# A planner's estimates and constants set anew in an attention and feed-forward kernel on one core

## The chip, the cores and the metric

The kernel runs on one core of a Trainium2 chip. A core has TensorE (PE, matmuls; PEld is its weight load), VectorE (DVE), ScalarE (ACT), GpSimd (POOL) and SyncE (SP), whose queue issues every DMA of this kernel. The metric is the device time of one execution in microseconds (us); lower is better.

## What is computed

```python
# B, H, Sl, Sg, D = 8, 8, 512, 32, 64
k_all, v_all = concat([k_g, k_l]), concat([v_g, v_l])
out_g = softmax(q_g @ k_all.T / 8) @ v_all                 # 32 global queries see everything
s_ll  = q_l @ k_l.T / 8, where |i - j| <= 32, else -1e9    # local queries: a window
out_l = softmax([q_l @ k_g.T / 8, s_ll]) @ v_all           # and the 32 global keys
x = concat([out_g, out_l]).reshape(B * 544, 512)
h = x @ w_in                                               # 512 -> 2048
g = h * tanh(softplus(h))                                  # mish
return g @ w_out                                           # 2048 -> 512
```

Everything is float32 outside. Inside, most products are made from two 16-bit or reduced parts (high and low), so that one float32 product is three matmuls (hi x hi, hi x lo, lo x hi).

## The kernel before

**Tiling.** Batches go from 0 to 7, head pairs (hp) from 0 to 3 in each, and four tiles of 128 queries (t) in each pair: 128 attention units. A unit computes scores `s` (two matmul groups, one for each head), the masked row maximum `P, nm` (DVE, L614), the exponential (ACT, L623), a high and a low part `ph` (ACT or DVE, L307, and DVE, L642), a DMA transpose to `pt` (SP, L467), and the product with v, `U` (PE, L659). After four units `x` (DVE, L669) is normalised, split into `xs` and transposed by DMA into `xh` and `xl`, which hold a whole batch. Each head pair also has the global queries: `g`, `gmx`, `gP`, `gph`, `gpt`, `gu`.

The feed-forward part works on blocks of 256 rows (two for each batch) in eight steps each: `h` (PE, L788, 24 matmuls, two halves of 12), mish into `e` (ACT, L831), two 16-bit parts `G` (DVE, L309 and L844), and `o` (PE, L856, 12 matmuls). Both h and o need prepared weights.

**The weights' way in.** The weights arrive as 64-bit words, 32 tiles of 512 KB: 0 to 15 are w_in, 16 to 31 w_out. Each is loaded (`w_load`) into a free place (`wraw` in a tile that is not yet in use, or a row of `W`). `w_bits` and `w_sum` make float32 from it: DVE shifts (L384), ACT takes the low word to `wr` (L386), DVE ors (L393), POOL adds (L395). `w_stat` multiplies each tile by itself on PE (`ws`, L405). After 16 tiles `w_norm` reduces: DVE `wd, wm` (L412), POOL's all-reduce `wp` (L416), DVE, ACT Ln and Exp (L418, L419), DVE scales `iw, sw`. Then `w_split` makes high and low parts of each of eight tiles: scaling (L307 or L309), high part, low part, the last on DVE for five tiles (L440) and on POOL for the other eleven (L445).

**The order.** Nothing is issued as it is written. Every step is added to a planner with its engine, an estimate of its time and a priority; `order` runs a list schedule over these estimates, and the instructions are then issued in the order of the estimated starts, one fixed queue for each engine. An engine takes what can start first, and of those ready the one of least priority number. A step's number is its place in the program, plus `late`, or `PER` = 37 times a `slot` where one is given. Estimates and constants thus set nothing on the chip but the order. Waits on the chip are for semaphores only, so a step that is late holds all that is queued behind it on its engine.

The constants of the weights' way in are slots: `CONV1 + RATE1 * k` and `CONV2 + RATE2 * (k - 16)` for the conversion of tile k, `AHEAD_DMA` by how many slots its load goes before it, `FIRST` and `STEP` for the splits. `LATE_K`, `LATE_L`, `LATE_B` and `LATE_V` push back the keys, the loads of k and q, the attention, and the values of batch 1.

Of the kernel before, what the change touches and what calls it, by code (L numbers as in the profile page):

```python
# [50 lines left out]
class Plan:  # L51
# [81 lines left out]
    def order(self):  # L133
        N = len(self.tasks)
        left, users = [0] * N, [[] for _ in range(N)]
        for n, t in enumerate(self.tasks):
            both = t[2] | t[3]
            left[n] = len(both)
            for d in both:
                users[d].append(n)  # L140
        free = dict.fromkeys((PE, DVE, ACT, POOL, DMA), 0)
        queue = {e: [] for e in free}
        start, done, on = [None] * N, [0] * N, [None] * N
        columns = {}

        def tensor(t, ns, rows):

            while ns > 1e-6:
                k = int(t / self.TICK + 1e-9)
                slow = 1 if columns.get(k - 1, 0) >= self.COLUMNS else 2  # L150
                d = min(ns * slow, (k + 1) * self.TICK - t)
                columns[k] = columns.get(k, 0) + d / slow * 2.4 * rows
                ns -= d / slow
                t += d
            return t

        def enter(n):
            engs, fn, deps, after, new, pri, rows, table = self.tasks[n]
            for e, ns in engs:
                t = max([done[d] + (self.NEXT[e] if on[d] == e else self.HOP) for d in deps] + [start[a] for a in after] + [0])  # L160
                bisect.insort(queue[e], (pri, n, ns, t))

        def first(e):

            best = None
            for pri, n, ns, t in queue[e]:
                t = max(t, free[e]) + (self.TABLE if e == ACT and self.tasks[n][7] not in (None, self.table) else 0)
                e0 = self.tasks[n][0][0][0]
                if e0 != e and free[e0] <= t + self.LOYAL:
                    continue  # L170
                if best is None or t < best[0]:
                    best = (t, pri, e, n, ns)
                    if t == free[e]:
                        break
            return best

        for n in range(N):
            if not left[n]:
                enter(n)
        for _ in range(N):  # L180
            t, pri, e, n, ns = min(c for c in map(first, free) if c)
            start[n], on[n] = t, e
# [32 lines left out]
def attn_mish_kernel(ctx: ExitStack, tc: tile.TileContext, qt, kt, qt0, kt0, vm, vg, qg, w1, w2, consts_in, out, w64):  # L215
# [73 lines left out]
    def pool(cols):  # L289
        return 2.39 * cols  # L290
# [38 lines left out]
    def wh(j, hl):  # L329
        return W[:, j + j // 8, hl * 512:(hl + 1) * 512].bitcast(F16)  # L330
# [26 lines left out]
    def words(k):  # L357
        return raw(k).rearrange("p (f w) -> p f w", w=2)
# [21 lines left out]
    def w_bits(k):  # L380
        if not w64:
            return
        f, key = lambda: wf(k).bitcast(I32), wkey(*HV[k])
        pl.add(DVE, 335, lambda: V.tensor_scalar(f(), words(k)[:, :, 1], 3, 0x3FFFFFFF, ALU.logical_shift_left, ALU.bitwise_and),  # L384
               r=[rawkey(k)], w=[key])
        pl.add(ACT, act(512), lambda: A.activation(out=X["wr", k], in_=words(k).bitcast(U32)[:, :, 0], func=AF.Copy,  # L386
                                                   scale=2.0 ** -29), r=[rawkey(k)], new=[("wr", ("wr", k))])

    def w_sum(k):
        if not w64:  # L390
            return
        f, key = lambda: wf(k).bitcast(I32), wkey(*HV[k])
        pl.add(DVE, 602, lambda: V.scalar_tensor_tensor(f(), words(k)[:, :, 1], -0x40000000, f(), ALU.bitwise_and, ALU.bitwise_or),  # L393
               r=[rawkey(k)], w=[key])
        pl.add(POOL, pool(512), lambda: G.tensor_tensor(f(), f(), X["wr", k], ALU.add), r=[("wr", k)], w=[key])  # L395

    def w_stat(k):

# [10 lines left out]
    def w_norm(w):  # L409

        m, p = ("wm", w), ("wp", w)
        pl.add(DVE, 210, lambda: V.tensor_tensor_reduce(out=X["wd", w][:, 0, :128],  # L412
                                                        in0=X["ws", w][:, :128], in1=ident, scale=1.0,
                                                        scalar=0.0, op0=ALU.mult, op1=ALU.add, accum_out=X[m]),
               r=[("ws", w), "consts"], new=[("wm", m), ("ob", ("wd", w))])
        pl.add(POOL, 600, lambda: G.partition_all_reduce(X[p], X[m], 128, RED.add), r=[m], new=[("p2", p)])  # L416
        pl.add(DVE, 70, lambda: V.tensor_scalar(X[p], X[p], TINY * TINY, None, ALU.max), w=[p])
        pl.add(ACT, 94, lambda: A.activation(out=X[p], in_=X[p], func=AF.Ln, bias=0.0, scale=1.0), w=[p], table="exp")  # L418
# [13 lines left out]
    def w_split(j):  # L432

        parted.add(j)
        w = j // 8
        f, c, k = W[:, j + j // 8 + 1, :], sw[:, w:w + 1], ("W", j + j // 8 + 1)
        hi, lo = [wslot(j), "hi"], [wslot(j), "lo"]
        if j < 8 - ON_POOL:
            pl.add([(ACT, act(1024)), (DVE, dve2(1024))], 0, lambda e: scaled(e, wh(j, 0), f, c), r=[k, ["sw", w]], w=[wslot(j)])
            pl.add(DVE, dve(1024), lambda: V.scalar_tensor_tensor(wh(j, 1), f, c, wh(j, 0), ALU.mult, ALU.subtract),  # L440
                   r=[k, ["sw", w], hi], w=[lo])
        else:
            pl.add([(ACT, act(1024)), (DVE, dve2(1024))], 0, lambda e: scaled(e, f, f, c), r=[["sw", w]], w=[k])
            pl.add([(ACT, act(1024)), (DVE, dve2(1024))], 0, lambda e: copy(e, wh(j, 0), f), r=[k], w=[wslot(j)])
            pl.add(POOL, pool(1024) * 0.9, lambda: G.tensor_tensor(wh(j, 1), f, wh(j, 0), ALU.subtract), r=[k, hi], w=[lo])  # L445


    LO, HI = slice(0, 64), slice(64, 128)
# [15 lines left out]

    def turn(kib, dst, src, r, w=(), new=()):

        pl.add(DMA, kib * 5, lambda: nc.sync.dma_start_transpose(dst(), src()), r=r, w=w, new=new)  # L467

    def b_load(b, what=None):
        if what == "g":  # L470
# [18 lines left out]
    def b_scale(b):  # L489

        m, p, sv = ("vmx", b), ("p2", b), ("sv", b)
        pl.add(POOL, 600, lambda: G.partition_all_reduce(X[p], X[m][:, 5:6], 128, RED.max), r=[m], new=[("p2", p)])
# [526 lines left out]
    RATE2 = 0.519  # L1019
    FIRST1 = 10.551  # L1020
    STEP1 = 0.114
    FIRST2 = 14.027
    STEP2 = 0.833
    AHEAD_DMA = 3.119
    LATE_K = 11.02
    LATE_L = 158.572
    LATE_B = 8.569
    LATE_V = 0.0

    def weights():  # L1030
        for k in range(32):
# [114 lines left out]
```

## Time and profile before

| | |
|---|---|
| time, median of 3 runs | 1021.27 us (1020.48 to 1023.16) |
| the profiled execution's own time | 1018.93 us |
| its span, first to last instruction | 1017.1 us |
| PE busy | 925.7 us, 91% |
| DVE, ACT busy | 668.5 us (66%), 680.9 us (67%) |
| POOL busy | 82.2 us, 8% |
| mean granted TensorE clock | 0.973 |
| DMA moved | 134.65 MB, of which 63.55 MB read from HBM |

A row of a timeline reads: start and length in us, engine, line, operation, output<-input, shape, count, and in brackets the idle time of the engine just before and what ended it. A row of a group ends with its count, its busy time, the mean ns of one, and the idle time before. A row of the waits gives the engine and line that waited, for whom, the sum, the number of times and the longest.

### The profile page before, as it was taken

Reading aid. Unit: us, or ns where it says so; the run is one execution under the profiler, and the core shown is the slowest. Engines: PE = TensorE matmul, PEld = TensorE weight load, DVE = VectorE, ACT = ScalarE, POOL = GpSimd, SP = SyncE. Lnnn points to the kernel's source line nnn. Section 1 sums busy time; section 2 is a strip of 40 time slices with the busy share of each in tenths; the row PEclk is TensorE's granted clock in tenths of the full one; section 3 lists DMA queues with packets and bytes.
Section 4 is the critical chain, followed back from the end, with each engine's and each line's share of the span. In section 5 each row is a group of like instructions: output and inputs, shape, how many; then the busy total and the mean of one; then the engine's idle time right before and its main releaser. Section 6 shows DMA issues by size and latency. Waiting matters only on the chain.

```text
span 1017.1 us, 20581 instructions
## 1 busy us (share of the span) xinstructions
PE 925.7 (91%) x7906; PEld 664.6 (65%) x7906; DVE 668.5 (66%) x1704; ACT 680.9 (67%) x1321; POOL 82.2 (8%) x62
## 2 busy tenths in 40 slices
PE   3455696899999999999999999999999999999996
PEld 2233475566776777677777777777777777666663
DVE  6977796887766767776677666767676655322221
ACT  3465566777897788878878888788878888211110
POOL 3725231410000000000000000000000000000000
PEclk9997588999999999999999999999999999999999
DMA  9847982587758664766557665666676544100000
GB/s 333 228 111 175 262 259 63 112 180 189 168 104 180 144 143 113 177 148 143 123 153 161 134 133 129 155 135 141 117 165 127 123 81 77 42 1 22 1 22 21
DMA packets 231802, 134.65 MB, mean 132 GB/s; under 512 B 197528, under 2 KB 209048, under 8 KB 230680
## 3 DMA queue, kind: packets, MB, share of 16 engines
q1 hardware_dynamic: 231704, 133.34, 57.1%
q8 instruction: 62, 1.02, 0.4%
q14 instruction: 36, 0.29, 0.1%
HBM read 63.55 MB, written 8.91 MB: 71 GB/s over the span
## 4 chain that ended last, share of the span: by engine, by line
PE 65%; DVE 12%; DMA 8%; ACT 4%; issue 3%; SPq 1%; POOL 0%; ACTq 0%; DVEq 0%
PE o L856 28%; PE h L788 26%; PE s L608 4%; PE U L659 3%; DMA vraw<-in_vm 3%; DMA pt<-ph 2%; PE g L697 2%; DMA gpt<-gph 2%; PE gu L745 1%; DVE vmx L481 1%; DVE P L614 1%; DVE ph L642 1%; DVE G L309 1%; SPq L296 1%; DVE kl L546 1%
## 5 line engine op out<-in xcount | busy, mean ns | idle before, releaser
L856 PE MATMUL o<-W,G 128*128 128x512 f16 x1632 | 389.8, 379 | 0.3 <-POOL W L445 0.3
L788 PE MATMUL h<-xh,W 128*128 128x256 f16 x2048 | 379.0, 275 | 5.1 <-ACT e L831 5.1
L788 PEld LDWEIGHTS <-W 128*128 128x128 f16 x3264 | 311.2, 98 | 68.6 <-issue 5.3
L788 PE MATMUL h<-xl,W 128*128 128x256 f16 x1024 | 281.0, 274 | 0.0
L856 PEld LDWEIGHTS <-G 128*128 128x128 f16 x1632 | 156.9, 98 | 144.1 <-issue 0.6
L831 ACT ACTIVATE e<-h,c 128x512 f32<-128x512 f32 (+1 forms) x137 | 92.6, 683 | 117.5 <-PE h L788 116.6
L623 ACT ACTIVATE P<-P,nm 128x192 f32<-128x192 f32 (+1 forms) x256 | 117.8, 460 | 41.5 <-DVE nm L614 40.3
L309 DVE TENSOR_SCALAR G<-e,c 128x512 f16<-128x512 f32 x129 | 63.9, 495 | 118.5 <-ACT e L831 118.4
L614 DVE CUSTOM_DVE_ANT_0 P<-s,consts 128x192 f32<-128x192 f32 (+1 forms) x256 | 90.1, 367 | 68.1 <-PE s L608 57.7
L642 DVE SCALAR_TENSOR_TENSOR ph<-P,ph 128x384 f16<-128x384 f32 (+1 forms) x128 | 78.0, 611 | 80.1 <-ACT ph L307 79.3
L844 DVE SCALAR_TENSOR_TENSOR G<-e,c,G 128x512 f16<-128x512 f32 (+1 forms) x137 | 102.0, 745 | 3.4
L831 ACT ACT_TABLE_LOAD x79 | 101.4, 1283 | 1.4
L623 ACT ACT_TABLE_LOAD x74 | 94.9, 1283 | 1.3
L659 PEld LDWEIGHTS <-pt 96*128 96x128 f16 (+1 forms) x1536 | 59.3, 101 | 33.5 <-DMA pt<-ph 26.9
L307 ACT ACTIVATE ph<-P 128x384 f16<-128x384 f32 (+1 forms) x128 | 69.7, 548 | 16.3 <-DMA pt<-ph 13.2
L659 PE MATMUL U<-va,pt 128*128 128x64 f16 (+1 forms) x768 | 59.4, 199 | 19.7 <-DMA pt<-ph 19.7
L608 PE MATMUL s<-ks,qs 128*128 128x192 f32 (+1 forms) x216 | 71.4, 353 | 1.4 <-DVE qs L538 0.9
L659 PE MATMUL U<-vc,pt 96*128 96x64 f16 x768 | 58.7, 198 | 0.0
L718 ACT ACTIVATE gP<-g,gmx 64x288 f32<-64x288 f32 x64 | 30.4, 476 | 37.5 <-DVE gmx L713 37.4
L395 POOL TENSOR_TENSOR W<-W,wr 128x512 int32<-128x512 int32 x32 | 48.8, 1535 | 79.0 <-DVE W L393 40.1
L608 PE MATMUL s<-kl,qs 128*128 128x192 f32 (+1 forms) x216 | 54.2, 274 | 0.0
L405 PE MATMUL ws<-W 128*128 128x128 bf16 x128 | 17.7, 286 | 37.4 <-POOL W L395 37.3
(103 smaller groups left out, 1024.3 us busy)
## 6 DMA issues: line engine op xcount, KB each, us to landing
kraw<-in_kt SPq DMA_DIRECT2D x27, 640.0 KB, 4.7
qraw<-in_qt SPq DMA_DIRECT2D x27, 512.0 KB, 3.8
W<-in_w SPq DMA_DIRECT2D x19, 512.0 KB, 7.1
out<-ob SPq DMA_DIRECT2D x34, 256.0 KB, 2.6
vraw<-in_vm SPq DMA_DIRECT2D x8, 1024.0 KB, 6.0
wraw<-in_w SPq DMA_DIRECT2D x13, 512.0 KB, 5.9
vc<-vf SPq DMA_DIRECT2D x32, 128.0 KB, 2.3
va<-vf SPq DMA_DIRECT2D x32, 96.0 KB, 2.3
```

Of the source, the lines that this page charges most:

```text
L307: A.activation(out=dst, in_=src, func=AF.Copy, scale=c)
L309: V.tensor_scalar(dst, src, c, None, ALU.mult)
L395: pl.add(POOL, pool(512), lambda: G.tensor_tensor(f(), f(), X["wr", k], ALU.add), r=[("wr", k)], w=[key])
L608: T.matmul(X[s][:, :w], X[qs][:, h, t * 128:(t + 1) * 128], X[k][:, h, c0:c0 + w], start=(i == 0), stop=(i == 1))
L614: pl.add(DVE, 69 + 1.04 * w, lambda: V.tensor_tensor_reduce(out=X[P][:, h, :w], in0=X[s][:, :w], in1=mask[:, m0:m0 + w], scale=-SCALE, sca ...
L623: pl.add(ACT, 160 + 0.832 * w + 93, lambda: A.activation(out=X[P][:, h, :w], in_=X[P][:, h, :w], func=AF.Exp, bias=X[nm], scale=-1.0, accu ...
L642: pl.add(DVE, dve(n), lambda: V.scalar_tensor_tensor(p_part(X[ph], t, 1), p_src(X[P], t), PSC, p_part(X[ph], t, 0), ALU.mult, ALU.subtract ...
L659: T.matmul(X[u][:, t, h, :], X[pt][:k, p * 4 + h * 2 + c, :], X[vx][:k, t, vl, h * 64:(h + 1) * 64], start=(n == 0), stop=(n == 5))
L788: T.matmul(X[h][:, f * TB:(f + 1) * TB], wh(i, wl)[:, off:off + 128], X[x][:, d, o:o + TB], start=(n == 0), stop=(n == 11))
L831: chain(blk, i, ACT, 571, lambda a, z: A.activation(out=X[e][:, a:z], in_=hv(blk, i)[:, a:z], func=AF.Mish, bias=0.0, scale=X[c][:, 0:1]), ...
L844: chain(blk, i, DVE, 602, lambda a, z: V.scalar_tensor_tensor(gp(1, blk, i)[:, a:z], X[e][:, a:z], X["c", blk][:, 2:3], gp(0, blk, i)[:, a ...
L856: T.matmul(X[o], gp(g, blk, i)[:, f, t * 128:(t + 1) * 128], wh(8 + i, wl)[:, f * 512:(f + 1) * 512], start=(i == 0 and n == 0), stop=(i = ...
```

## The change

The planner's estimates change (in ns): POOL's add of a conversion to 1400 (1224 before), its all-reduces to 4500 (600), its subtract for low parts to 2230 (2203), DVE's shift to 360 (335) and or to 680 (602), a DMA transpose to 8 for each KiB (5). A DMA's time is now counted in one stream of bytes, with up to 4 us of it ahead, in place of one transfer after the other; DVE beside a busy POOL is charged 0.6 of the overlap, not 0.5. Five constants of the weights' way in and of batch 1 change, and the loads of w_in get slots of their own. No instruction is added or removed but what follows from the order: which of ACT and DVE takes a step that either may do, and ACT's table loads, 159 before and 156 now.

```diff
-    DMA_IN, DMA_OUT, DMA_MIN = 1650, 900, 650
+    DMA_IN, DMA_OUT, DMA_MIN, DMA_AHEAD = 1300, 600, 620, 4000
...
-                ns += 0.5 * min(ns, free[POOL] - t)
+                ns += 0.6 * min(ns, free[POOL] - t)
             if e == DMA:
-                free[e] = t + max(ns, self.DMA_MIN)
-                done[n] = t + self.DMA_IN + ns + self.DMA_OUT
+                moved = max(moved, t) + ns
+                free[e] = max(t + self.DMA_MIN, moved - self.DMA_AHEAD)
+                done[n] = moved + self.DMA_IN + self.DMA_OUT
...
-        pl.add(POOL, pool(512), lambda: G.tensor_tensor(f(), f(), X["wr", k], ALU.add), r=[("wr", k)], w=[key])
+        pl.add(POOL, 1400, lambda: G.tensor_tensor(f(), f(), X["wr", k], ALU.add), r=[("wr", k)], w=[key])
...
-        pl.add(POOL, 600, lambda: G.partition_all_reduce(X[p], X[m], 128, RED.add), r=[m], new=[("p2", p)])
+        pl.add(POOL, 4500, lambda: G.partition_all_reduce(X[p], X[m], 128, RED.add), r=[m], new=[("p2", p)])
...
-    FIRST2 = 14.027
+    FIRST2 = 9.91
     STEP2 = 0.833
-    AHEAD_DMA = 3.119
-    LATE_K = 11.02
-    LATE_L = 158.572
-    LATE_B = 8.569
-    LATE_V = 0.0
+    LOAD1 = -1.233
+    LOADS1 = 0.2
+    AHEAD_DMA = 7.72
+    LATE_K = 33.326
+    LATE_L = 168.71
+    LATE_B = 9.983
+    LATE_V = 399.689
...
         if a == "w":
+            pl.slot = LOAD1 + LOADS1 * n
             w_load(n)
+            pl.slot = None
```

What this does to the order is shown at three places. In names the first index (the batch, or the block of a feed-forward step) is left out: `P_1_1` is head pair 1, unit 1 of its batch, `x_3` head pair 3; a last number only counts buffers. Line numbers of the new kernel are two higher here.

VectorE at the first weight norm, before: three steps of work stand between the reduction `wd, wm` and the row `wp` that waits for POOL's all-reduce.

```order
L393 SCALAR_TENSOR_TENSOR W<-wraw_338,W 128x512
L642 SCALAR_TENSOR_TENSOR ph_72<-P_0_2_130,ph_72 128x2x224
L412 ISA wd_400,wm_399<-ws_200,consts 128x128
L412 ISA wm_399 128x1
L614 ISA P_1_1_403,nm_1_1_0_404<-s_1_1_0_232,consts 128x224
L614 ISA nm_1_1_0_404 128x1
L614 ISA P_1_1_403,nm_1_1_1_410<-s_1_1_1_270,consts 128x224
L614 ISA nm_1_1_1_410 128x1
L642 SCALAR_TENSOR_TENSOR ph_73<-P_0_3_157,ph_73 128x2x192
L417 TENSOR_SCALAR wp_406<-wp_406 128x1
```

The same place now, right behind the rows of `wd, wm`:

```order
L644 SCALAR_TENSOR_TENSOR ph_72<-P_1_0_327,ph_72 128x4x96
L386 TENSOR_SCALAR W<-wraw_426 128x512
L616 ISA P_1_3_507,nm_1_3_0_508<-s_1_3_0_430,consts 128x192
L616 ISA nm_1_3_0_508 128x1
L395 SCALAR_TENSOR_TENSOR W<-wraw_426,W 128x512
L616 ISA P_1_3_507,nm_1_3_1_532<-s_1_3_1_449,consts 128x192
L616 ISA nm_1_3_1_532 128x1
L669 TENSOR_SCALAR rs_1_539<-sums_1_334 128x8
L670 RECIPROCAL rs_1_539<-rs_1_539 128x8
L712 TENSOR_REDUCE gmx_1_557<-g_1_0_534 64x1
L644 SCALAR_TENSOR_TENSOR ph_73<-P_1_1_406,ph_73 128x2x224
L419 TENSOR_SCALAR wp_496<-wp_496 128x1
```

A conversion, the sums `rs`, a gmx and a second ph came in between, and tiles 16 and 17 are converted ahead of `wd`, where 15 was the last.

ScalarE at the second weight norm, before: it stands behind the mish results 4 to 7 of block 0 and behind the vgf and vf of batch 1, with a table load for Ln, one for Exp and one back to mish.

```order
L831 ACTIVATE e_5_1491<-h_5_1413,c_452 128x512
L512 ACTIVATE vgf_1553<-vgraw_936,sv_1533 128x128
L307 ACTIVATE vf_0_1555<-vraw_878,sv_1533 128x4x128
L307 ACTIVATE vf_1_1574<-vraw_878,sv_1533 128x4x128
L831 ACTIVATE e_6_1578<-h_6_1493,c_452 128x512
L831 ACTIVATE e_7_1583<-h_7_1518,c_452 128x512
L418 ACT_TABLE_LOAD
L418 ACTIVATE wp_1511<-wp_1511 128x1
L419 ACT_TABLE_LOAD
L419 ACTIVATE wp_1511<-wp_1511 128x1
L307 ACTIVATE W<-W,sw 128x1024 x2
L300 CAST W<-W 128x1024
```

Now:

```order
L302 CAST qgh_1314<-qgraw_1291 128x768
L420 ACTIVATE wp_1271<-wp_1271 128x1
L720 ACTIVATE gP_0_1332,gs_0_1333<-g_0_0_1259,gmx_0_1289 64x288
L421 ACTIVATE wp_1271<-wp_1271 128x1
L720 ACTIVATE gP_0_1332,gs_0_1333<-g_0_1_1273,gmx_0_1289 64x256
L833 ACT_TABLE_LOAD
L833 ACTIVATE e_0_1359<-h_0_1276,c_609 128x512
L309 ACTIVATE W<-W,sw 128x1024
L833 ACTIVATE e_1_1387<-h_1_1299,c_609 128x512
L302 CAST W<-W 128x1024
L309 ACTIVATE W<-W,sw 128x1024
L833 ACTIVATE e_2_1425<-h_2_1369,c_609 128x512
```

The norm moved ahead of the first mish, with no table load of its own, and the splits of w_out run between the first mish results. On TensorE the first o then follows 8 half steps of h; before, it followed all of block 0 and two steps of block 1.

VectorE at the end of batch 0, before: `x_3` of batch 0 stands eight rows ahead of this piece, which holds two conversions' rows and the parts of keys 1 of batch 1 (`ks_1`, `kl_1`).

```order
L384 TENSOR_SCALAR W<-W 128x512
L614 ISA P_0_2_1171,nm_0_2_0_1172<-s_0_2_0_1159,consts 128x224
L614 ISA nm_0_2_0_1172 128x1
L393 SCALAR_TENSOR_TENSOR W<-W 128x512
L614 ISA P_0_2_1171,nm_0_2_1_1179<-s_0_2_1_1169,consts 128x224
L614 ISA nm_0_2_1_1179 128x1
L302 CAST ks_1_1185<-kraw_1_1128 128x1280
L642 SCALAR_TENSOR_TENSOR ph_73<-P_0_1_1154,ph_73 128x2x224
L546 TENSOR_TENSOR kl_1_1209<-kraw_1_1128,ks_1_1185 128x640
```

Now these parts and the low part of queries 1 stand ahead of `x_3`, which comes 23 rows behind the last row of this piece:

```order
L304 CAST ks_1_1047<-kraw_1_768 128x1280
L680 TENSOR_TENSOR xs_2_1040<-x_2_1027,xs_2_1040 128x512
L712 TENSOR_REDUCE gmx_3_1042<-g_3_1_1034 64x1
L616 ISA P_0_0_1076,nm_0_0_0_1077<-s_0_0_0_1044,consts 128x192
L616 ISA nm_0_0_0_1077 128x1
L715 TENSOR_SCALAR gmx_3_1042<-gmx_3_1042 64x1
L644 SCALAR_TENSOR_TENSOR ph_72<-P_3_2_988,ph_72 128x2x224
L548 TENSOR_TENSOR kl_1_1091<-kraw_1_768,ks_1_1047 128x640
L669 TENSOR_SCALAR rs_3_1099<-sums_3_876 128x8
L540 TENSOR_TENSOR qs_1_1031<-qraw_1_789,qs_1_1031 64x1024
```

Of the conversions, 26 stood ahead of `x_3` of batch 0 before and 31 do now. On SP's queue, 28 loads of weights stood ahead of the last transposes into `xh` of batch 0, and all 32 do now.

More of the change, by code (lines that the diff above doesn't have):

```diff
@@ L144, in order @@
         columns = {}
+        moved = 0
         def tensor(t, ns, rows):
@@ L383, in w_bits @@
         f, key = lambda: wf(k).bitcast(I32), wkey(*HV[k])
-        pl.add(DVE, 335, lambda: V.tensor_scalar(f(), words(k)[:, :, 1], 3, 0x3FFFFFFF, ALU.logical_shift_left, ALU.bitwise_and),
+        pl.add(DVE, 360, lambda: V.tensor_scalar(f(), words(k)[:, :, 1], 3, 0x3FFFFFFF, ALU.logical_shift_left, ALU.bitwise_and),
                r=[rawkey(k)], w=[key])
@@ L392, in w_sum @@
         f, key = lambda: wf(k).bitcast(I32), wkey(*HV[k])
-        pl.add(DVE, 602, lambda: V.scalar_tensor_tensor(f(), words(k)[:, :, 1], -0x40000000, f(), ALU.bitwise_and, ALU.bitwise_or),
+        pl.add(DVE, 680, lambda: V.scalar_tensor_tensor(f(), words(k)[:, :, 1], -0x40000000, f(), ALU.bitwise_and, ALU.bitwise_or),
                r=[rawkey(k)], w=[key])
-        pl.add(POOL, pool(512), lambda: G.tensor_tensor(f(), f(), X["wr", k], ALU.add), r=[("wr", k)], w=[key])
+        pl.add(POOL, 1400, lambda: G.tensor_tensor(f(), f(), X["wr", k], ALU.add), r=[("wr", k)], w=[key])
     def w_stat(k):
@@ L444, in w_split @@
             pl.add([(ACT, act(1024)), (DVE, dve2(1024))], 0, lambda e: copy(e, wh(j, 0), f), r=[k], w=[wslot(j)])
-            pl.add(POOL, pool(1024) * 0.9, lambda: G.tensor_tensor(wh(j, 1), f, wh(j, 0), ALU.subtract), r=[k, hi], w=[lo])
+            pl.add(POOL, 2230, lambda: G.tensor_tensor(wh(j, 1), f, wh(j, 0), ALU.subtract), r=[k, hi], w=[lo])
     LO, HI = slice(0, 64), slice(64, 128)
@@ L465, in turn @@
     def turn(kib, dst, src, r, w=(), new=()):
-        pl.add(DMA, kib * 5, lambda: nc.sync.dma_start_transpose(dst(), src()), r=r, w=w, new=new)
+        pl.add(DMA, kib * 8, lambda: nc.sync.dma_start_transpose(dst(), src()), r=r, w=w, new=new)
     def b_load(b, what=None):
@@ L491, in b_scale @@
         m, p, sv = ("vmx", b), ("p2", b), ("sv", b)
-        pl.add(POOL, 600, lambda: G.partition_all_reduce(X[p], X[m][:, 5:6], 128, RED.max), r=[m], new=[("p2", p)])
+        pl.add(POOL, 4500, lambda: G.partition_all_reduce(X[p], X[m][:, 5:6], 128, RED.max), r=[m], new=[("p2", p)])
         def go():
```

## The prediction

> **What bounds the kernel now.** I read the page's slices first, then busy time by stretches, then TensorE's waits, then VectorE's, and last the chain of waits and the instructions in order of time. The first fence cuts the span where the work changes character: at the first h matmul, and at the first score matmul of batch 2.
>
> ```profile
> core 0: us, PE busy (x) PEld busy (x) DVE busy (x) ACT busy (x) POOL busy (x), PEclk, DMA share, GB/s
> 0.00:132.02 132.02, 70.63 (x460) 44.31 (x461) 104.26 (x241) 69.44 (x169) 54.81 (x42) 0.84 0.82 223
> 132.02:237.29 105.27, 91.05 (x796) 66.06 (x796) 88.00 (x205) 71.28 (x141) 25.62 (x15) 0.95 0.66 152
> 237.29:1017.10 779.81, 764.03 (x6653) 554.19 (x6651) 476.21 (x1260) 540.19 (x1012) 1.75 (x5) 1.00 0.52 114
> ```
>
> From 237.29 on TensorE is busy 764 of 780 us: that stretch is its own work. In the first stretch TensorE works 70.6 of 132.0 us and VectorE 104.3, with GpSimd at 54.8. So the start is held by VectorE and what it waits for, the second stretch by a mixture, the third by TensorE. Both orders put the same 1,200 matmuls ahead of the first score matmul of batch 2. Whatever the change does to the time is therefore almost wholly the moment at which that matmul starts, 237.29 now:
>
> ```profile
> 132.02 0.39 PE L788 MATMUL h<-xh,W 128*128 128x256 f16 x1
> ...
> 138.90 0.65 PE L697 MATMUL g<-ks,qgraw 128*64 128x256 f32 x2
> ...
> 167.08 0.37 PE L788 MATMUL h<-xh,W 128*128 128x256 f16 x1 [5.12 <-ACT e L831]
> ...
> 175.07 0.25 PE L659 MATMUL U<-va,pt 96*128 96x64 f16 x3
> ...
> 237.29 0.44 PE L608 MATMUL s<-ks,qs 128*128 128x192 f32 x1
> ```
>
> **Second stretch: what it must cost.** Where TensorE is dense, the chain of waits gives its pace (start, length, what):
>
> ```profile
> 251.10 0.44 PE s L608 x4
> ...
> 251.90 2.59 PE o L856 x12
> ...
> 254.92 1.19 PE g L697 x12
> ...
> 257.41 3.93 PE h L788 x36
> 261.34 0.36 PE U L659 x12
> ```
>
> In the new order there stand between the first h and that score matmul 336 h, 144 o, 156 U, 45 gu, 48 s and 36 g. At 3.93/36, 2.59/12, 0.36/12 (gu like U), 0.44/4 and 1.19/12 this is 36.7 + 31.1 + 4.7 + 1.4 + 5.3 + 3.6 = 82.7 us. The old stretch holds 28 ws and one g more, some 2.9, so 85.6 of its 105.27 us were work at full pace and 19.7 were lost. The waits name most of it:
>
> ```profile
> PE h L788 <- ACT e L831: 5.1, 1, 5.1
> PE U L659 <- DMA pt<-ph: 5.1, 6, 1.7
> PE ws L405 <- POOL W L395: 3.0, 2, 2.6
> ```
>
> With 1.2 of smaller waits that is 14.4 (14.2 by busy time). The other 5.3 is slow pace: 48 h take 6.9 us from 132.02 and 8.0 from 167.08, against 5.2 dense, so 1.7 and 2.8 are lost behind the two idle times.
>
> What the change does here, edit by edit. The weights' loads of w_out move up (AHEAD_DMA), so all 32 tiles are converted ahead of the first h, where 28 ws matmuls (seven tiles) stood behind it: the 3.0 goes. The all-reduce of the second weight norm is now answered before the first mish, and ScalarE's order puts four mish results ahead of the first vf and vgf of batch 1, which wait for that batch's all-reduce and now hold up e behind them: the 5.1 goes, and with it the second slow pace, 2.8. The transposes pt are as many as before: 5.1 stays, with the 1.2 of small ones. In place of the waits removed comes the chain from the norm to the first o, now on the path. I walk it from the first h at T: the last ws stand one set of g (about 2 us by the row at 138.90, an estimate) ahead of T; the answer of the all-reduce comes 5.3 us after VectorE's row (below), T + 3.7; Ln, Exp, two gP and a table load bring the first mish to its end at about T + 7.4. TensorE is then still with four h halves (6.9 at the slow pace) and two s. The first tile's scale, copy and GpSimd's subtract end near T + 12.6, and eight halves of h end at about the same time. So nothing large is exposed; I put 3 us on what such a walk misses. Loss: 5.1 + 1.2 + 1.7 + 3 = 11.0, and the stretch 82.7 + 11.0 = 93.7 us, 11.6 less than now. Bounds: 8 if the 3 is nothing, 19.7 if all that goes comes back.
>
> ```profile
> 167.62 1.28 ACT L418 ACT_TABLE_LOAD   x1
> 168.92 0.20 ACT L418 ACTIVATE wp<-wp 128x1 f32<-128x1 f32 x1
> ```
>
> The table load costs its 1.28 and no more: the next activation starts 0.02 later. The Trainium skill (ScalarE: Activation LUTs, section What ACT_TABLE_LOAD costs) adds a drain and puts every switch at about 2.66 us. By that rule the first mish would end 1.4 later, TensorE would wait about 1 us more, and the time would be 1013.4; the trace does not agree here, so I leave it out.
>
> **First stretch: when h can start.** It needs all of batch 0's attention, so VectorE's row x of the last head pair. Its waits and its costliest rows until then (of one kind: mean ns):
>
> ```profile
> DVE wp L417 <- POOL wp L416: 4.2, 1, 4.2
> DVE ph L642 <- ACT ph L307: 3.3, 1, 3.3
> DVE P L614 <- PE s L601: 3.0, 3, 2.1
> ...
> DVE wd L412 <- PE ws L405: 1.8, 1, 1.8
> ...
> DVE W L384 <- DMA W<-in_w: 0.9, 1, 0.9
> ...
> L393 DVE SCALAR_TENSOR_TENSOR W<-W 128x512 int32<-128x512 int32 x17 | 19.3, 1141 | 0.1
> L384 DVE TENSOR_SCALAR W<-W 128x512 int32<-128x512 int32 x17 | 10.7, 631 | 0.9 <-DMA W<-in_w 0.9
> ...
> L309 DVE TENSOR_SCALAR vf<-vraw,sv 128x512 f16<-128x512 f32 x1 | 2.0, 1953 | 0.4 <-PE gu L745 0.4
> ...
> L309 DVE TENSOR_SCALAR W<-W,sw 128x1024 f32<-128x1024 f32 x2 | 1.5, 750 | 0.0
> ```
>
> Added ahead of that row: five conversions (31 instead of 26) at 1.14 + 0.63 = 1.77 each, 8.9; one ks, two kl and one qs of batch 1, which stood behind it:
>
> ```profile
> L302 DVE CAST ks<-kraw 128x1280 fp32r<-128x1280 f32 x16 | 14.6, 913 | 0.2
> L546 DVE TENSOR_TENSOR kl<-kraw,ks 128x640 fp32r<-128x640 f32 x54 | 44.3, 821 | 0.2 <-ACT ks L300 0.2
> L538 DVE TENSOR_TENSOR qs<-qraw,qs 64x1024 fp32r<-64x1024 f32 x27 | 33.0, 1223 | 0.8
> ```
>
> 0.9 + 1.6 + 1.2 = 3.8. Moved off to ScalarE: one vf (2.0) and two scalings of W (1.5); one gph comes over, about 0.5. Net 9.7 us more work. Against it, the order puts work into the waits.
>
> ```profile
> 52.53 0.08 DVE L412 DVE_READ_ACCUMULATOR2_ANT wm<- 128x1 f32 x1
> ...
> 57.94 0.15 DVE L417 TENSOR_SCALAR wp<-wp 128x1 f32<-128x1 f32 x1 [4.24 <-POOL wp L416]
> ```
>
> The all-reduce answers 5.3 us after the first row. VectorE has 1.3 us of work to put there now; in the new order a conversion, two row maxima, a gmx and a ph more, about 3.2: 1.9 of the 4.2 goes. The 1.8 of wd goes (two more conversions stand ahead of it), and the 0.9 on a W load. Of the 3.3 and the 3.0, queue effects that I cannot follow row by row, I take half, 3.1; none and all are the bounds. One g product of 0.65 moves ahead of the first h. So h starts at 132.0 + 9.7 + 0.7 - 1.9 - 1.8 - 0.9 - 3.1 = 134.7, between 131.6 and 137.8 by these bounds.
>
> What a conversion costs depends on GpSimd:
>
> ```profile
> 35.25 0.68 DVE L393 SCALAR_TENSOR_TENSOR W<-W 128x512 int32<-128x512 int32 x1
> 35.85 0.41 DVE L384 TENSOR_SCALAR W<-W 128x512 int32<-128x512 int32 x1
> ...
> 38.30 1.63 DVE L393 SCALAR_TENSOR_TENSOR W<-W 128x512 int32<-128x512 int32 x1
> 38.08 1.31 POOL L395 TENSOR_TENSOR W<-W,wr 128x512 int32<-128x512 int32 x1 [0.69 <-DVE W L393]
> ```
>
> Alone the OR takes 0.68; beside GpSimd's add it ends 0.54 after the add does. The Trainium skill (SBUF — State Buffer, section SBUF: two separate sides) says that the pair of ports is locked for a whole instruction and the loser blocks fully. By that rule, with nothing overlapped, a conversion costs 0.41 + 0.68 + 1.31 = 2.4, five cost 12.0, and the time is 1015.5; the rows agree with a lock, but the means above show part of it overlapped, and I go by them.
>
> **The sum.** The score matmul of batch 2 starts at 134.7 + 93.7 = 228.4 instead of 237.29: 8.9 us earlier. The third stretch has the same matmuls at the same pace; its interleaving differs a little and I cost that at nothing, since TensorE is busy for 98% of it. The profiled execution took 1018.93 (1.83 around its span); less 8.9 that is 1010.0. The median shown, 1021.27, is 2.3 above the profiled one; from it the forecast is 1012.4.
>
> **The rivals.** (1) Larger gain: every wait of the first stretch that I halved goes, and the 3 us in the second are nothing. Then h starts at 131.6 and the stretch takes 90.7: 222.3, 15 us gained, 1006.3. For it: the new estimates for the all-reduce (4.5 us against 5.3 seen, 0.6 before) and for GpSimd's add (1.4 against 1.31) are nearer to the rows. Against: VectorE would have to be busy almost without gaps.
>
> (2) No change that can be measured: the moved conversions are paid in full and the freed waits return elsewhere. h at 138 and, with 15 us lost, 97.7 in the second stretch: 235.7, 1019.7. For it: VectorE and GpSimd are the resource of the start, and moving work does not shrink it.
>
> (3) Slower: the weights' loads now stand ahead of the transposes in SP's one queue.
>
> ```profile
> DMA  9847982587758664766557665666676544100000
> ...
> pt<-ph SPq DMA_TRANSPOSE x128, 3.1
> ...
> 117.45 6.33 DMA pt<-ph
> ```
>
> Ahead of the last xh transpose stand 32 weight loads instead of 28, and two k and q loads that came later. A transpose beside such loads took 6.33 in the chain, against 3.1 at the median. If the last ten units of batch 0 each paid 3.2 more, with two ph buffers hiding a third, that is some 21 us on the first stretch, h at 156 and 249.7 for the score matmul: 1033.7. It decides from where it costs more than 12 us (six units), since 8.9 are gained elsewhere; six to seven units give 1025 to 1027. Against it: in the first row, the page's busy tenths of the 16 DMA engines in slices of 25 us, the third slice (51 to 76 us) has a 4 between an 8 and a 7, and the loads move into that gap.
>
> **How the numbers follow.** Forecast 0.50 (its own range 1007 to 1018), larger gain 0.22, no change 0.15, slower 0.13. A change below 0.3%, some 3 us, cannot be told from none in this kernel. Faster 0.72, same 0.15, slower 0.13. The range 1003 to 1022 leaves out most of the slower case and the far end of the larger gain.
>
> **What would show it.** In the changed profile the first h should start between 131 and 138, with all L405 groups ahead of it; the 5.1 us wait of h for e should be gone; the wait of wp for the first all-reduce should be about 2; the first score matmul of batch 2 should start near 228, and TensorE should be dense behind it. I am wrong if h starts after 143, if o waits for GpSimd's W by more than 5 us, or if the third stretch grows by more than 3 us.

## The result, and the profile after

The changed kernel takes 1035.50 us (median of four runs, 1032.37 to 1036.92), the kernel before 1021.44 in the same session: 1.013 times as long, 95% interval 1.0112 to 1.0147. The forecast was 1012.4, so the sign was wrong. The profiled execution took 1032.37 with a span of 1030.6; the stretches below are of this one. Cut where the prediction cut (first h matmul, first score matmul of batch 2), the busy times by stretch of the changed kernel:

```profile
core 0: us, PE busy (x) PEld busy (x) DVE busy (x) ACT busy (x) POOL busy (x), PEclk, DMA share, GB/s
0.00:150.63 150.63, 75.12 (x490) 48.11 (x491) 117.25 (x260) 75.02 (x180) 58.53 (x46) 0.56 0.79 220
150.63:246.44 95.81, 86.72 (x766) 63.93 (x766) 75.33 (x175) 68.00 (x134) 20.59 (x11) 0.96 0.61 130
246.44:1030.60 784.16, 762.81 (x6653) 554.68 (x6651) 475.67 (x1264) 540.06 (x1012) 3.27 (x5) 1.00 0.52 114
```

| stretch | before | predicted | after |
|---|---|---|---|
| to the first h | 132.02 | 134.7 | 150.63 |
| first h to first score matmul of batch 2 | 105.27 | 93.7 | 95.81 |
| from there on | 779.81 | 779.8 | 784.16 |

The premise held that both orders put the same number of matmuls ahead of that score matmul (460 + 796 before, 490 + 766 after, 1,256 each, where the prediction has 1,200). The gain of the second stretch came (9.5 of 11.6 us). The loss is in the first, 18.6 us where 2.7 were forecast, with 4.4 in the third. What VectorE waits for in the first stretch (total, times, longest):

```profile
DVE xs L680 <- ACT xs L302: 9.0, 2, 8.3
DVE vgf L516 <- ACT vgf L514: 7.9, 1, 7.9
DVE P L616 <- PE s L603: 6.3, 4, 4.8
DVE W L386 <- DMA W<-in_w: 3.0, 1, 3.0
...
DVE wp L419 <- POOL wp L418: 1.1, 1, 1.1
```

The first two are new, 16.9 us together. Both end on ScalarE, which had stood idle. ScalarE's rows around the wait for `vgf`, the earlier of the two, of the changed kernel:

```profile
15.70 0.67 ACT L388 ACTIVATE wr<-wraw 128x512 int32<-128x512 uint32 x1 [0.25 <-DMA wraw<-in_w]
16.34 0.50 ACT L720 ACTIVATE gP<-g,gmx 64x288 f32<-64x288 f32 x1
...
24.79 0.68 ACT L388 ACTIVATE wr<-wraw 128x512 int32<-128x512 uint32 x1 [7.42 <-POOL W L397]
25.37 0.39 ACT L514 ACTIVATE vgf<-vgraw,sv 128x128 f16<-128x128 f32 x1
```

and the same place before:

```profile
14.90 0.65 ACT L386 ACTIVATE wr<-wraw 128x512 int32<-128x512 uint32 x1
15.45 0.39 ACT L512 ACTIVATE vgf<-vgraw,sv 128x128 f16<-128x128 f32 x1
15.74 1.32 ACT L307 ACTIVATE vf<-vraw,sv 128x512 f16<-128x512 f32 x2
23.76 0.69 ACT L386 ACTIVATE wr<-wraw 128x512 int32<-128x512 uint32 x1 [6.70 <-POOL W L395]
```

ScalarE stands until 24 in both, at the third `wr`: there are two `wr` buffers, and the first comes free when GpSimd has added tile 0. Before, `vgf` and two `vf` stood ahead of the third `wr` in the queue and were done, and VectorE worked on. After, the third `wr` stands directly ahead of `vgf`, and VectorE stands with ScalarE. Why GpSimd adds so late, its rows after and then before:

```profile
12.87 0.65 POOL L494 PARTITION_ALL_REDUCE p<-vmx  x1 [7.43 <-DVE vmx L489]
23.51 2.48 POOL L397 TENSOR_TENSOR W<-W,wr 128x512 int32<-128x512 int32 x2 [9.99 <-issue]
```

```profile
13.55 0.65 POOL L492 PARTITION_ALL_REDUCE p<-vmx  x1 [8.12 <-DVE vmx L487]
22.42 2.98 POOL L395 TENSOR_TENSOR W<-W,wr 128x512 int32<-128x512 int32 x2 [8.21 <-DVE W L393]
```

Behind an all-reduce of 0.65 us GpSimd does nothing for 10 us, and the view names no one that it waited for ("issue"). For some 2 of the 10 us its add still lacked VectorE's part of tile 0 (L395, ended at 15.7); for the other 7.8 it lacked nothing that the trace shows. Before, the stand (this time of doing nothing) is there too, 8.2 us, put down to a VectorE row that had ended at 16.0, 6.5 us ahead of the add. The second new wait is the same thing behind the all-reduce of the first weight norm (GpSimd, then ScalarE, of the changed kernel):

```profile
67.69 0.40 POOL L418 PARTITION_ALL_REDUCE wp<-wm  x1 [5.89 <-DVE ph L644]
75.13 2.49 POOL L397 TENSOR_TENSOR W<-W,wr 128x512 int32<-128x512 int32 x2 [7.04 <-issue]
```

```profile
76.42 0.68 ACT L388 ACTIVATE wr<-W 128x512 int32<-128x512 uint32 x1 [7.67 <-POOL W L397]
77.00 0.61 ACT L302 CAST xs<-x 128x512 f16<-128x512 f32 x1
```

What stands between is a change of GpSimd's configuration on its sequencer, ahead of the first ordinary add behind an all-reduce (name, count, duration in ns, first and last start):

```profile
L397 POOLq MODIFY_POOL_CONFIG  x4: 83/83/83, 13.4 to 68.1; - x4
```

The Trainium skill (GPSIMD Engine Reference, section 2.1 Instruction dispatch) says that this instruction can bring in new code, and that the first call of freshly loaded code pays about 6 us with nothing visible in the profile. The trace agrees in kind and shows 7.0 and 10.0 us on the way back to ordinary work. No row shows what fills that time; that the all-reduce brings it on is tested below. An engineer who had read that sentence beside the row at 22.42 would have had the rival that came true.

A second thing stands out in the page after: the granted clock (first row before, second row after).

```profile
PEclk9997588999999999999999999999999999999999
```

```profile
PEclk8555559899999999999999999999999999999998
```

Half speed in the slices from 26 to 155 us; before it was half in one slice. That makes a theory of its own, so the experiments carry three: **A**, GpSimd's stand behind each all-reduce, passed on by a `wr` ahead of what VectorE needs; **B**, TensorE's half clock makes the scores late; **C**, VectorE has more work ahead of the first h (117.3 us busy against 104.3).

### The profile page after: what moved, and what is told of

It is laid out like the page before. It is cut to its first block, busy times and chain, and to the rows that moved or that the text cites. A ratio compares the mean times of both kernels' runs of the same rounds, so it can differ in the third digit from the quotient of the medians.

```text
span 1030.6 us, 20569 instructions
## 1 busy us (share of the span) xinstructions
PE 924.6 (90%) x7906; PEld 666.7 (65%) x7906; DVE 668.2 (65%) x1697; ACT 683.1 (66%) x1325; POOL 82.4 (8%) x62
## 4 chain that ended last, share of the span: by engine, by line
PE 63%; DVE 13%; DMA 8%; ACT 6%; issue 5%; SPq 3%; POOL 2%; DVEq 0%; POOLq 0%; ACTq 0%
PE o L858 26%; PE h L790 26%; PE s L610 4%; SPq L298 3%; DMA vraw<-in_vm 3%; PE U L661 3%; PE g L699 2%; DMA gpt<-gph 2%; PE gu L747 1%; ACT L833 1%; DVE ph L644 1%; POOL W L447 1%; DVE W L395 1%; DVE P L616 1%; DVE vmx L483 1%
## 5 line engine op out<-in xcount | busy, mean ns | idle before, releaser
L311 DVE TENSOR_SCALAR G<-e,c 128x512 f16<-128x512 f32 (+1 forms) x130 | 62.4, 480 | 119.5 <-ACT e L833 119.0
L846 DVE SCALAR_TENSOR_TENSOR G<-e,c,G 128x512 f16<-128x512 f32 (+1 forms) x137 | 105.8, 772 | 4.0 <-ACT G L309 0.8
L833 ACT ACT_TABLE_LOAD x78 | 100.1, 1283 | 1.6 <-DVE G L846 0.2
L625 ACT ACT_TABLE_LOAD x75 | 96.2, 1283 | 1.4
L397 POOL TENSOR_TENSOR W<-W,wr 128x512 int32<-128x512 int32 x32 | 45.8, 1438 | 71.3 <-DVE W L395 31.8
```

The lines of the kernel that those rows point to most:

```text
L311: V.tensor_scalar(dst, src, c, None, ALU.mult)
L397: pl.add(POOL, 1400, lambda: G.tensor_tensor(f(), f(), X["wr", k], ALU.add), r=[("wr", k)], w=[key])
L625: pl.add(ACT, 160 + 0.832 * w + 93, lambda: A.activation(out=X[P][:, h, :w], in_=X[P][:, h, :w], func=AF.Exp, bias=X[nm], scale=-1.0, accu ...
L833: chain(blk, i, ACT, 571, lambda a, z: A.activation(out=X[e][:, a:z], in_=hv(blk, i)[:, a:z], func=AF.Mish, bias=0.0, scale=X[c][:, 0:1]), ...
L846: chain(blk, i, DVE, 602, lambda a, z: V.scalar_tensor_tensor(gp(1, blk, i)[:, a:z], X[e][:, a:z], X["c", blk][:, 2:3], gp(0, blk, i)[:, a ...
```

## The experiments

### Three rows moved in the changed order; one row moved in the old one

```
 (changed kernel, behind order())
+ move wr 2 behind vf(0,1); wr 19 behind gP(0,1); wr 20 behind wr 19
```

> The changed order with three steps of one queue moved by hand: ScalarE's wr of tile 2 goes behind the first two vf, its wr of tiles 19 and 20 behind the gP of head pair 1. All else is as in the changed kernel. Theory A (GpSimd stands still for 7 to 10 us behind each all-reduce; a wr that waits for its next add holds vgf and xs behind it on ScalarE, and VectorE behind these): the waits of 7.9 and 8.3 us go. VectorE then meets some of what it does later sooner, so I expect 8 to 16 us back: first h at 135 to 143 instead of 150.6, time 1020 to 1027. Theory B (TensorE at half its clock from 16 to 151 us makes the scores late): the clock is not touched, first h stays within 3 us of 150.6, time 1033 to 1037. Theory C (VectorE has 13 us more work ahead of the first h): nothing moves, as in B.

Measured: 1027.34 us (before 1020.36 in the session; ratio 1.0074, 1.0053 to 1.0095), just above the 1020 to 1027 of theory A: 7.0 us slower than the kernel before instead of 14.1. First h at 141.35, 9.3 earlier; second stretch 95.9, third 785.6. VectorE's waits up to the first h (line numbers are shifted by the lines that an edit adds, here and in the runs below):

```profile
DVE P L621 <- PE s L608: 6.5, 4, 4.9
DVE gs L733 <- ACT gP L725: 4.8, 1, 4.8
...
DVE xs L685 <- ACT xs L307: 0.9, 2, 0.7
```

The wait for `vgf` is gone and that for `xs` is 0.9; 4.8 came back at `gs`. The converse, in the kernel before, with nothing else touched:

```
 (kernel before, behind order())
+ move wr 2 ahead of vgf(0)
```

> The kernel before with a single row of one queue moved: ScalarE's wr of tile 2, which stands behind vgf and the first two vf, goes ahead of vgf, as in the changed kernel. Nothing else differs. Theory A: the row waits for GpSimd's first add behind the all-reduce (22.4 us here), vgf follows at about 24.5, and VectorE, which reads vgf at 16.2 now, stands still for about 8 us; some of it comes back, since VectorE waits 4.2 us for wp and 3.3 for ph later: first h 4 to 8 us later, at 136 to 140, time 1024 to 1029. Rival (the stand is taken up by VectorE's other waits, so that the row's place does not matter): 1020 to 1022, first h within 1.5 us of 132.0.

Measured: 1029.75 us (before 1021.27; ratio 1.0084, 1.0070 to 1.0098). First h at 140.34, 8.3 later, a little more than expected; the other two stretches 106.0 and 780.0, within 1 us of before. ScalarE and then VectorE at that place:

```profile
24.53 0.67 ACT L390 ACTIVATE wr<-wraw 128x512 int32<-128x512 uint32 x1 [9.74 <-DMA ks<-in_kt]
25.10 0.39 ACT L516 ACTIVATE vgf<-vgraw,sv 128x128 f16<-128x128 f32 x1
```

```profile
25.52 0.35 DVE L518 SCALAR_TENSOR_TENSOR vgf<-vgraw,sv,vgf 128x128 f16<-128x128 f32 x1 [9.98 <-ACT vgf L516]
```

One row of 0.67 us, moved ahead of three others in its queue (`vgf` and two `vf`), costs 8.5 us of the whole. (The releaser named, a DMA, is not it: by its place this `wr` needs the add of tile 0, as in the kernel before.) That is theory A. C has no part in it: VectorE is busy for 103.97 us up to the first h, against 104.26 before. B is settled below.

### The all-reduces taken out

```
- G.partition_all_reduce(X[p], X[m], 128, RED.add)     (and RED.max of X[m][:, 5:6])
+ G.tensor_tensor(X[p], X[m], X[m], ALU.add)           (and of X[m][:, 5:6])
```

These two kernels leave out the reduction across partitions; they serve to time the rest.

> The changed order with each of GpSimd's ten all-reduces replaced by an ordinary add of the same column to itself, on the same engine and at the same place; the reduction across partitions is left out. Theory A (the all-reduce is dear because GpSimd changes its code before and behind it): GpSimd's stand of 10 us at 13 us and of 7 us at 68 us go, and the waits of 7.9 and 8.3 with them: first h at 133 to 138, time 1015 to 1021. Theory B (half clock): at most 3 us. Theory C (work of VectorE): the time stays within 4 us of 1035.

> The kernel before with the same replacement of the ten all-reduces; the reduction across partitions is left out. Theory A: the old order hid the stand behind the first all-reduce and most of the second, so it gains only the wait of wp, 4.2, and some of what follows: first h at 125 to 129, time 1013 to 1018. The difference between the two orders, 14 us with all-reduces, should fall to between -3 and +6. Theories B and C: the difference between the orders stays at 10 to 14 us.

Measured: changed order 1018.43 (before 1020.36; ratio 0.9982, 0.9972 to 0.9992), old order 1013.41 (0.9935, 0.9915 to 0.9956). First h at 135.68 and 126.93. GpSimd of the changed order, where no change of configuration is left ahead of the adds:

```profile
13.02 0.50 POOL L494 TENSOR_TENSOR p<-vmx 128x1 f32<-128x1 f32 x1 [7.56 <-DVE vmx L489]
15.95 1.40 POOL L397 TENSOR_TENSOR W<-W,wr 128x512 int32<-128x512 int32 x1 [2.43 <-DVE W L395]
```

The first add starts at 15.95 instead of 23.51. So the all-reduces, with GpSimd's way to them and back, cost the changed order 16 to 17 us (from 14.1 slower than the kernel before to 1.9 faster) and the old one 7, and the two orders without them are 5 us apart, not 14. Of the 18.6 us by which h came later, 9.9 go with the all-reduces (15.0 less 5.1); 8.75 remain between the two orders without them, where VectorE is busy for 119.25 against 105.36 us. So theory C has a part too; which of the moved rows cost it was not tried. Busy times up to the first h, of the changed order without all-reduces and of the run with the estimates alone (below):

```profile
0.00:135.68 135.68, 74.84 (x490) 47.97 (x490) 119.25 (x260) 74.55 (x180) 59.98 (x48) 0.57 0.88 244
```

```profile
0.00:148.88 148.88, 73.60 (x481) 46.72 (x481) 114.70 (x251) 74.64 (x175) 55.79 (x45) 1.00 0.79 222
```

At a granted clock of 0.57 h starts at 135.7; at 1.00 it starts at 148.9. Nor does the clock go with the time among executions of one kernel: of the ten of the changed order without all-reduces, the three whose mean clock was below 0.94 took 1017.46 to 1018.96 us, the five above 0.99 took 1017.52 to 1020.53. And TensorE's pace up to the first h is the same at either value: four `ws` take 0.61 us at a granted clock of 0.50 (changed kernel) and at 1.00 (estimates alone), and less only later. This settles theory B.

```profile
24.82 0.61 PE L407 MATMUL ws<-W 128*128 128x128 bf16 x4 [9.67 <-POOL W L397]
```

```profile
25.33 0.61 PE L407 MATMUL ws<-W 128*128 128x128 bf16 x4 [7.66 <-POOL W L397]
...
155.04 0.39 PE L407 MATMUL ws<-W 128*128 128x128 bf16 x4
```

### The halves of the change, and one estimate

The estimates and the DMA model alone, with all constants as before:

> One half of the change alone: the new estimates and the new model of the DMAs, with all constants of the weights' way in as before. In the order that comes out the wr of tile 2 stands ahead of vgf, as in the changed kernel, and from batch 3 on every engine's order is that of the changed kernel. Theory A (a wr that waits for GpSimd behind an all-reduce holds what VectorE needs): the wait for vgf, 7 to 8 us, is there, the one for xs is smaller, since xs stands later; first h at 138 to 146. The third stretch (from the first score matmul of batch 2) is 783 to 786 us, as in the changed kernel: its order is the same. Time 1024 to 1033. Rival (the constants do the harm, the estimates are nearer to the truth and help): 1012 to 1020.

Measured 1031.64 us (before 1021.02; ratio 1.0113, 1.0085 to 1.0141): first h at 148.88, with a wait of 8.6 us for `vgf`; second stretch 101.1, third 783.3. The time, the wait and the third stretch are as expected; h is 2.9 us beyond its bound, in an execution (1035.12) that was the longest of its four. The constants alone (six in the diff, and the slots of the w_in loads), with all estimates as before:

> The other half alone: the new constants, with the old estimates. From batch 3 on the order is that of the kernel before. vgf stands ahead of all wr; the wr of tile 19 stands ahead of four W and of xs behind the second all-reduce. Theory A: no wait for vgf, one of 4 to 8 us for xs or W; the second all-reduce as in the run with 600 ns, with h waiting for e there; first h at 138 to 146, third stretch 779 to 781, time 1026 to 1038. Rival (the estimates do the harm): 1012 to 1022.

Measured 1040.94 us (ratio 1.0199, 1.0174 to 1.0223), worse than expected. First h is at 136.09, within the prediction's bounds, with no wait for `vgf` but 7.6 for `xs`; the third stretch takes 784.6, where 779 to 781 was expected, and the second 119.7. There TensorE, GpSimd and ScalarE read:

```profile
171.64 0.37 PE L788 MATMUL h<-xh,W 128*128 128x256 f16 x1 [17.95 <-ACT e L831]
```

```profile
148.95 1.39 POOL L492 PARTITION_ALL_REDUCE p<-vmx  x1 [4.62 <-DVE vmx L487]
158.17 2.11 POOL L445 TENSOR_TENSOR W<-W 128x1024 f16<-128x1024 f32 x1 [7.84 <-issue]
```

```profile
160.32 1.04 ACT L300 CAST W<-W 128x1024 f16<-128x1024 f32 x1 [7.88 <-POOL W L445]
...
170.91 1.27 ACT L831 ACTIVATE e<-h,c 128x512 f32<-128x512 f32 x2
```

The same stand again, behind the all-reduces of the second norm and of batch 1: a copy of W waits for GpSimd, and the mish e, which the dense TensorE needs, stands behind it. A third place where it can hurt, which the changed order avoids since its estimate of 4.5 us lets e go first. My expectation had this as a few us. Alone the halves cost 10.6 and 19.9 us, together 14.1: they do not add. The changed kernel with that one estimate at 600 ns again:

> The changed kernel with one estimate set back: the all-reduce 600 ns again instead of 4500, both lines; all else as in the changed kernel. In the order that comes out vgf stands ahead of the wr of tile 1, and wr of tile 19 still stands ahead of xs. Theory A: the 7.9 us wait for vgf goes, the one of 8 us behind the second all-reduce stays: first h at 140 to 146, time 1025 to 1030. Theory B: no change, 1033 to 1037, unless the clock comes back. Theory C: within 3 us of 1035.

Measured 1042.92 us (before 1020.36; ratio 1.0228, 1.0204 to 1.0251); a miss. The wait for `vgf` did go and the one for `xs` stayed (7.1), as expected, with h at 146.40; but h then waits 9.1 us for e, and the second stretch takes 108.4. So neither 0.6 nor 4.5 us is right for this all-reduce: the answer comes 0.4 us after its start (67.69, and wp's next row at 68.12), and GpSimd is away for 7 to 10. With the old DMA model in the changed kernel:

> The changed kernel with the old model of the DMAs (1650, 900 and 650 ns, each transfer by itself, transposes 5 ns per KiB); everything else new. vgf and vf stand ahead of the wr of tile 2, and xs ahead of the second all-reduce's answer; the wr of tile 19 still stands ahead of the W splits. Theory A: the two large waits of VectorE go, 3 to 5 us come back at W: first h at 137 to 144. The order from batch 3 on is close to that of the kernel before, so if the DMA model is what lengthens the third stretch, it is 779 to 782 us, else 784 to 786. Time 1019 to 1028. If the half clock were the cause: 1033 to 1037.

Measured 1030.58 us (before 1021.02; ratio 1.0106, 1.0072 to 1.0140), above the range expected. First h is at 138.89 as expected, but the stand is not gone: a `wr` now stands ahead of the second `vf`, and behind the second all-reduce ahead of a `ph`, and VectorE waits 6.9 and 7.8 us for these two. Second stretch 107.3 (h waits 5.8 for e), third 782.6, between the two cases; so it does not decide what lengthens the third.

### A planner that knows of the stand

```
+    TO_LIB, FROM_LIB = 5700, 8000
     ...
+                if e == POOL and (self.tasks[n][7] == "lib") != lib:
+                    t = max(t, free[e] + (self.FROM_LIB if lib else self.TO_LIB))
     (both all-reduces: 600 ns, table="lib")
```

> The kernel before with one thing more in the planner: GpSimd needs 5.7 us to come to an all-reduce and 8 us to come back from it to ordinary work (with 600 ns for the all-reduce itself), as the trace shows. Only the order changes, and only in the first 170 us. Theory A: a planner that knows of the stand puts less behind it, but the old order hid most of it already; what can be had at most is 7 us (the run without all-reduces), and I expect a third to two thirds: time 1014 to 1019. Rival: the constants were fitted to the old estimates, so any other order is worse: 1021 to 1030.

> The changed kernel with the all-reduce at 600 ns and, in the planner, 5.7 us for GpSimd to come to an all-reduce and 8 us to come back. vgf and both first vf stand ahead of the wr of tile 1, and the second all-reduce comes later in the order, with xs of both first head pairs ahead of it. Theory A: VectorE's waits for vgf and xs go, first h at 134 to 142, second stretch 95 to 105, third 783 to 785: time 1016 to 1028. If constants fitted to 4.5 us do harm with any other estimate, as with 600 ns: 1035 to 1045.

Measured: on the kernel before 1015.98 us (before 1021.02; ratio 0.9956, 0.9943 to 0.9969), on the changed one 1024.41 (before 1020.95; ratio 1.0040, 1.0025 to 1.0055). Both as expected, but for the third stretch of the second (786.4). The first is the fastest full kernel here, 0.4% faster than before: first h at 127.74, in an execution (1019.57) that was the longest of its ten. In the second h is at 134.08 with no wait of VectorE for `vgf` or `xs`, and 7.4 us are lost in the second stretch, h for e.

### The reductions on TensorE

```
-        pl.add(POOL, 600, lambda: G.partition_all_reduce(X[p], X[m], 128, RED.add), ...)
+        pl.add(PE, mm(1, 400), lambda: T.matmul(X["ws", w][:, 128:129], ones, X[m], ...), ...)
     (the maximum, for batches 0 and 1: matmul with ident, DVE maximum, matmul with ones)
```

> The kernel before with the reductions across partitions of the weights' norms and of v in batches 0 and 1 taken from GpSimd to TensorE (a matmul with a matrix of ones for the sum; for the maximum a matmul with the unit matrix, VectorE's maximum over the row, and a matmul with ones). The result is the same; GpSimd has no all-reduce left before the last weights are done. Theory A: as in the run with the all-reduces replaced by adds, 7 us faster than before, first h at 125 to 129, time 1012 to 1017; no stand of GpSimd over 6 us that ends with no waiting for others. Rival (TensorE's queue waits for VectorE at the new matmuls, and the order shifts): 1019 to 1024.

> The changed kernel with the same four reductions on TensorE. Theory A: the waits for vgf and xs go; first h at 130 to 137, time 1013 to 1019, so between the run of the changed order with adds in place of all-reduces (1018.4) and the same of before (1013.4). Theory that the rest of the change is a gain by itself, as predicted: at or below 1010. If the order of the changed kernel is bad for other reasons: 1022 to 1035.

Measured: 1021.79 (before 1020.95; ratio 1.0005, 0.9991 to 1.0020) and 1036.95 us (1.0153, 1.0135 to 1.0172). First h came as expected, at 125.44 and 136.76, and the times did not: the second is as slow as the changed kernel, with h 13.9 us earlier. So an early first h is not kept of itself. The first run gave it back later: 107.0 in the second stretch and 788.7 in the third, with the third's order of TensorE and of the DMA queue from batch 2 on the same as in the kernel before; what lengthened it stays open. The other took 112.0 us for the second stretch (h waits 8.2 for e). In both, VectorE's first row maxima start at 14 us instead of 6 to 7, since the score matmuls stand behind the new ones for the maximum of v, so this is no clean trial of the idea.

## Why the prediction was wrong, point by point

**First stretch, the step that failed.** "The all-reduce answers 5.3 us after the first row" priced the answer alone. That GpSimd cannot work for 7 to 10 us behind it stood in the trace of before (13.55, 22.42, and ScalarE's 6.70 for POOL at 23.76), hidden by the releaser named. So no term of the sum, and no rival, asked what stands behind `wr` on ScalarE. The waits that I did name behaved: wp 4.2, wd 1.8, W load 0.9, ph 3.3 and s 3.0, together 13.2, became 1.1, 0, 3.0, 1.0 and some 1.5, or 6.6: less by 6.6, forecast 7.7. The missing term is the 16.9 of new waits. VectorE's account of the 18.6 us is 13.0 more work, 16.9 of the two new waits, and 11.2 less of all others, part of it likely because what VectorE used to wait for had come by then. The runs put the net price for h at 8.3 us (one `wr` moved in the old order), 9.3 (three moved back in the changed one) and 9.9 (all-reduces out of both). Of the three signs of being wrong that the prediction named two came, h after 143 and a third stretch longer by more than 3; o waited for no W of GpSimd.

**The work ahead of h** was forecast at 9.7 us and is 13.0, but not where I put it. The conversions, 8.9 by my sum, grew from 47.0 to 48.3 us (28 rows each of L393 and L384 against 32, so four more and not five). Instead rows that used to run alone now run beside GpSimd: ph 577 to 715 ns, vf 749 to 1246, xs 680 to 1168, gph (L730) 1023 to 1256. One of them, with GpSimd's row beside it; it ends 0.55 us after the add does, as the OR did in the prediction:

```profile
27.01 1.75 DVE L563 SCALAR_TENSOR_TENSOR vf<-vraw,sv,vf 128x512 f16<-128x512 f32 x1
```

```profile
26.89 1.32 POOL L397 TENSOR_TENSOR W<-W,wr 128x512 int32<-128x512 int32 x1 [0.90 <-DVE W L395]
```

The mean cost of a conversion was the wrong unit: by these rows the overlap with GpSimd moved to others, and did not shrink. That is a reading of the rows; no run tested it.

**Second stretch.** 95.8 against 93.7, and in part by luck: the 5.1 us wait of h for e is 1.3 and the ws behind POOL are gone, as forecast, but pt, forecast to stay at 5.1, went from 4.9 to 2.0, and TensorE is busy for 86.7 us where 82.7 and 1.7 of slow pace were forecast. What "such a walk misses", forecast at 3, was one new wait of 5.3:

```profile
PE U L661 <- DMA va<-vgf: 5.3, 1, 5.3
PE U L661 <- DMA pt<-ph: 2.0, 2, 1.3
PE h L790 <- ACT e L833: 1.3, 1, 1.3
```

The walk held only by the estimate of 4.5 us, as the runs without it show (9.1 and 18.0 us for e).

**Third stretch.** Costed at nothing, it grew by 4.4, past my own bound of 3. TensorE waits there, before and then after:

```profile
PE U L659 <- DMA pt<-ph: 4.1, 6, 1.8
PE gu L745 <- DMA gpt<-gph: 1.3, 4, 0.4
```

```profile
PE h L790 <- ACT e L833: 7.5, 5, 1.6
PE gu L747 <- DMA gpt<-gph: 2.3, 4, 1.6
PE s L610 <- ACT gP L720: 1.5, 2, 0.9
```

Five waits of h for e, up to 1.6 us each, are new. They are in every run with the new estimates and the new DMA model (6.7 to 7.6 us), and the stretch takes 783.3 to 786.5 there. But six kernels with the old order (the same from batch 3 on) took 779.8 to 788.7, so how much of the 4.4 is the order's stays open.

**The rivals.** The slower one (13%) came true for another reason than its own: it had transposes wait behind weight loads, but U's wait for pt in the first stretch fell, before and then after:

```profile
PE U L659 <- DMA pt<-ph: 10.6, 6, 3.6
```

```profile
PE U L661 <- DMA pt<-ph: 2.8, 1, 2.8
```

**The table load and the shared ports.** A table load still costs 1283 ns in the mean, not the 2.66 us that the Trainium skill (ScalarE: Activation LUTs, section What ACT_TABLE_LOAD costs) gives. That VectorE can be held by GpSimd at a shared pair of ports, as the Trainium skill (SBUF — State Buffer, section SBUF: two separate sides) has it, agrees with the rows above. It may be part of the 8.75 us between the orders without all-reduces; the two new waits are not of this kind.

## What to carry to other kernels

When an engine's row starts late, look at whether the releaser named had long ended; if so, look for what that engine itself was doing, above all behind an instruction of another kind (here 7 to 10 us on GpSimd behind an all-reduce of 0.65). A stand on one engine costs less when what others need stands ahead, in each queue, of the row that waits for it (the all-reduces cost 7 us in the old order, 16 to 17 in the new); so for every moved row, ask which engine it can hold up and who reads the next row. And an estimate that lumps answer and occupancy into one number (0.6 or 4.5 us) is wrong for one of the two; two numbers gave, on the old constants, the only full kernel here that beat the one before. And an early start of one stage is no gain until the next keeps it: two runs had h near 136 us and still took 1037 and 1041.

## What the runs showed of the hardware that was not expected

GpSimd's way back from an all-reduce took 8.2, 10.0, 7.0 and 7.8 us in the rows above, counted from the end of the all-reduce, and its way to one 5.9; the 6 us of the Trainium skill (GPSIMD Engine Reference, section 2.1 Instruction dispatch) fit the second. The granted clock that the profile lists did not go with TensorE's pace: it was half from about 18 to 151 us in the changed kernel and full for the whole first stretch in the run with the estimates alone, and four `ws` took 0.61 us in both. What sets either was not tried.
